# Packing the columns of two attention blocks and widening the stationary slices of the scores to 128

## The chip, the core and the metric

The kernel runs on one core of a Trainium2 chip. A core has TensorE (matrix products; a matmul keeps one operand, the stationary one, in the array and streams the other, the moving one, through it), VectorE, ScalarE, GpSimd and SyncE, an on-chip memory of 128 partitions (SBUF), accumulation banks (PSUM) and DMA queues to HBM. The profile writes them PE (TensorE's matmuls), PEld (its loads of the stationary operand), DVE (VectorE), ACT (ScalarE), POOL (GpSimd) and SP (SyncE). The metric is the device time in microseconds (us); the value before is the median of four runs. One ns is a thousandth of a us.

## The reference

Two branches read the same layer-normalised input, and their outputs are added to the input. Branch A is attention in 64 segments of 32 tokens, each with 8 memory rows that come out of the segment before. Branch B is a mixing MLP. Cut to what matters here:

```
x  = A_x                                  # [1, 2048, 1024]
xn = layernorm(x)
# branch A, for each segment s of 32 tokens, 32 heads of 128:
h = concatenate([mem, xn[segment s]])     # 8 + 32 rows
q = h @ Wq ; k = h @ Wk ; v = h @ Wv
scores = where(mask, q @ k.T * scale, -1e9)
o = softmax(scores) @ v
o = o @ Wo
mem = o[:8]                               # goes on to segment s + 1
# result
x + A(xn) + B(xn)
```

## The kernel before

The first half of the kernel (to about 755 us) computes branch B, estimates of the memory rows, and the values V of all tokens, and stores V in HBM. At lines 595 to 601 a loop over eight groups of heads does the values: matmuls on PE, and casts of the results that take turns on ACT and DVE. In the passes `hg` = 1 to 4 of that loop (lines 606 to 614) the transposed input of attention block `b = hg` is gathered into the tile `hTs`: POOL clears it (`memset`, line 612), DVE copies token columns and memory columns into it (`fill`, lines 189 and 192), and POOL's queue stores it in the HBM scratch `hT_d[b]`.

The second half is the attention proper. The 64 segments are cut into five **blocks**, 0 to 4, run one after another, each in eight passes `hg` over groups of four heads. A block is a row of **tiles** (`tiles_of`): a tile is three segments (99 columns: 96 tokens and 3 memory columns; 106 columns in the first tile of block 0) or two (66 columns). Blocks 1 and 2 have four tiles of 99, 396 columns; block 0 has 403; blocks 3 and 4 have four tiles of 99 and one of 66, 462. The number of columns of a block is `nb`, a tile's first column is `c0`, its width `T`.

Blocks 0, 3 and 4 hold their tiles side by side. Blocks 1 and 2 hold each tile of 99 in a stretch of 104 columns, 416 in all, both in the gathered input and in the tiles QT and KT of queries and keys. What of a block depends on this is `rhs` (the moving operand of the projections) and `cols` (the columns of QT and KT), lines 634 to 649.

Per pass there are three kinds of PE work in this stage:

- **Projections** (`proj`, line 667): for each of eight outputs (four heads, Q then K), eight matmuls with a 128x128 weight stationary and the block's columns moving. ACT copies the result from PSUM to QT (line 675) or KT (line 673). In blocks 1 and 2 the moving operand and the copies go through a pattern of four runs of 99.
- **Scores** (`scores`, line 682): four matmuls per tile, one for each head, with the tile's `T` query columns stationary and its `T` key columns moving. DVE adds the mask (line 684), ACT takes the exponential (686), DVE sums, inverts and normalises (688 to 694), and a transposing DMA makes PT.
- **Outputs** (`outputs`, line 706): four matmuls per tile with `T` rows of V (128 columns) stationary and `T` columns of PT moving.

A block's share of the final product with Wo (`Out.piece`, line 725: 512 moving columns) is done in pieces during the next block.

The order on PE, SP and POOL is the order in which the program issues instructions. A running clock places the small work: `tick` adds an estimate that is computed from `nb`, and issues a due scores or outputs item after a projection of eight matmuls. `step`, the distance between scores items, is computed from `nb` as well. Scores of a pass are issued after all of the projections of that pass, that is, during the projections of the next; QT and KT have two buffers each.

In all there are 2,560 projection matmuls (512 a block), 704 scores matmuls (176 tiles times four) and 704 outputs matmuls.

Of the kernel before, what the change touches and what calls it, by code (L numbers as in the profile page):

```python
# [15 lines left out]
BF16 = mybir.dt.bfloat16  # L16
# [7 lines left out]
P = 128  # L24
S = 2048
D = 1024
KT = D // P
# [50 lines left out]
def kernel(  # L78
# [16 lines left out]
    nc = tc.nc  # L95
# [14 lines left out]
    R1_v = R1_d.rearrange("(n p) d -> p n d", p=P)  # L110
    xn_d = tc.dram_tile([S, D], BF16, name="xn_scratch")
    xn_v = xn_d.rearrange("(n p) d -> p n d", p=P)
    hT_d = {b: tc.dram_tile([P, KT * c], BF16, name=f"hT{b}_scratch") for b, c in ((1, 416), (2, 416), (3, 464), (4, 464))}
    V_d = tc.dram_tile([S, H * DH], BF16, name="V_scratch")
    Vr_d = tc.dram_tile([NQ + 1, H * DH], BF16, name="Vmem_scratch")

# [77 lines left out]
    with tc.manual_schedule(engines={mybir.EngineType.PE, mybir.EngineType.SP, mybir.EngineType.Pool}), ExitStack() as actx:  # L194
# [6 lines left out]
        with ExitStack() as bctx:  # L201
# [13 lines left out]
            with ExitStack() as hctx:  # L215
# [7 lines left out]
                with ExitStack() as p0:  # L223
# [109 lines left out]
                    ps = psum.tile([P, 512], F32, tag="mm", bufs=4, name="warm")  # L333
# [52 lines left out]
                with ExitStack() as p2:  # L386
                    ring = p2.enter_context(tc.tile_pool(name="p2ring", bufs=4))
                    for n in range(NT):
                        x1 = ring.tile([P, D], F32, tag="x1")
                        st = ring.tile([P, 2, 6], F32, tag="st")  # L390
                        for ch in range(2):
                            ps = psum.tile([P, 512], F32, tag="mm", bufs=4)
                            for k in range(KT):
                                o = 2 + n * P + SH[k]
# [5 lines left out]
                        a = ring.tile([P, 1], F32, tag="a")  # L400
# [12 lines left out]
            with ExitStack() as p3:  # L413
# [118 lines left out]
                for tb in range(4):  # L532
                    depth = 1 if tb < 2 else 2
                    for f in range(FT):
                        ps = psum.tile([P, 512], F32, tag="mm", bufs=4)
# [9 lines left out]
                    if tb == 3:  # L545
                        w3ctx.close()
                        early = actx.enter_context(tc.tile_pool(name="aearly", bufs=1, side="right"))
# [3 lines left out]
                    for j in range(4):  # L551
# [8 lines left out]
                        for ch in range(2):  # L560
                            ps = psum.tile([P, 512], F32, tag="mm", bufs=4)
# [16 lines left out]
            abig = actx.enter_context(tc.tile_pool(name="abig", bufs=1))  # L578
# [4 lines left out]
            for hg in range(8):  # L583
                cs_ = slice(hg * 512, (hg + 1) * 512)
                while len(wvs) < min(8, hg + 3):
                    load_wv()
                wv = wvs[hg]
                if 1 <= hg < 5:
                    nc.gpsimd.dma_start(wo_sb[:, (hg - 1) * 8:hg * 8, :], Wo_v[:, (hg - 1) * 8:hg * 8, :])
                for m4 in range(4):  # L590
                    Vs = vsp.tile([P, 4, 512], BF16, tag="Vs")
                    for j in range(4):
                        ps = psum.tile([P, 512], F32, tag="mm", bufs=4)
                        for k in range(KT):
                            nc.tensor.matmul(ps[:], xT[:, m4 * 4 + j, k, :], wv[:, k, :], start=(k == 0), stop=(k == KT - 1))  # L595
                        if j % 2 == 0:
                            nc.scalar.copy(Vs[:, j, :], ps[:])  # L597
                            if (hg, m4, j) == (7, 3, 2):
                                nc.scalar.activation(etab[:], ps[:, 0:1], ACTF.Exp, scale=0.0)
                        else:  # L600
                            nc.vector.tensor_copy(Vs[:, j, :], ps[:])  # L601
                    nc.sync.dma_start(V_d[m4 * 512:(m4 + 1) * 512, cs_].rearrange("(j p) c -> p j c", p=P), Vs[:])
                if hg == 1:
                    for t in pns:
                        nc.gpsimd.memset(t[:], 0.0)
                if 1 <= hg < 5:
                    b, (tl, nb) = hg, tiles_of(hg)
                    if b < 3:
                        for t in tl:
                            t["c0"] = 104 * t["i"]  # L610
                    hTs = abig.tile([P, KT, 464 if b > 2 else 104 * len(tl)], BF16, tag="oX", name=f"hTs{b}")
                    nc.gpsimd.memset(hTs[:], 0.0)
                    fill(hTs, tl, lambda j, b=b: xT[:, j])
                    nc.gpsimd.dma_start(hT_d[b][:], hTs[:].rearrange("p k c -> p (k c)"))
                if hg == 6:
                    first_w = [wtile(), wtile()]
                    for w, src in zip(first_w, (Wq_v, Wk_v)):
                        nc.sync.dma_start(w[:], src[:, :, 0:512])
                if hg == 7:
                    second_w = [wtile(), abig.tile([P, KT, 512], BF16, tag="oXb", name="wk1")]  # L620
                    for w, src in zip(second_w, (Wq_v, Wk_v)):
                        nc.sync.dma_start(w[:], src[:, :, 512:1024])
                if hg == 0:
                    tl, nb = tiles_of(0)
                    hTb0 = early.tile([P, KT, 408], BF16, tag="hTb0")
                    fill(hTb0, tl, lambda j: xT[:, j])
# [6 lines left out]
        qkv = actx.enter_context(tc.tile_pool(name="aqkv", bufs=2, side="right"))  # L633
        def block_setup(b):
            tl, nb = tiles_of(b)
            ntok = sum(t["ntok"] for t in tl)
            if b == 0:
                hTb, rhs = hTb0, lambda k: hTb0[:, k, :nb]
            else:
                nt = len(tl)  # L640
                hTb = early.tile([P, KT, 464 if b > 2 else 104 * nt], BF16, tag=f"hTb{b % 2}")
                nc.gpsimd.dma_start(hTb[:].rearrange("p k c -> p (k c)"), hT_d[b][:])
                if b > 2:
                    rhs = lambda k: hTb[:, k, :nb]
                else:
                    rhs = lambda k: hTb[:, k, :].rearrange("p (t c) -> p t c", t=nt)[:, :, 0:99]
                    for t in tl:
                        t["c0"] = 104 * t["i"]
            return dict(b=b, tiles=tl, nb=nb, ntok=ntok, rhs=rhs, cols=nb if b in (0, 3, 4) else 104 * len(tl))

        def load_values(B, V, hg):
            b, cs_ = B["b"], slice(hg * 512, (hg + 1) * 512)
# [7 lines left out]
                nc.sync.dma_start(V[w:w + n, i0:i0 + k, :], Vr_d[t["r0"]:t["r0"] + n * k, cs_].rearrange("(t j) c -> j t c", j=n))  # L660

        def proj(B, w, hh, dst, scale):
            nb, nt = B["nb"], len(B["tiles"])
            flat = B["b"] in (0, 3, 4)
            ps = psum.tile([P, 512], F32, tag="mm", bufs=4)
            for k in range(KT):
                nc.tensor.matmul(ps[:, :nb] if flat else ps[:, :nb].rearrange("p (t c) -> p t c", t=nt), w[:, k, hh * P:(hh + 1) * P], B["rhs"](k), start=(k == 0), stop=(k == KT - 1))  # L667
            if flat:
                o, i = dst[:, hh, :nb], ps[:, :nb]
            else:  # L670
                o, i = dst[:, hh, :].rearrange("p (t c) -> p t c", t=nt)[:, :, 0:99], ps[:, :nb].rearrange("p (t c) -> p t c", t=nt)
            if scale is None:
                nc.scalar.copy(o, i)  # L673
            else:
                nc.scalar.mul(o, i, scale)  # L675

        def scores(t, hg, QT, KTt):
            c0, T = t["c0"], t["T"]
            psS = apsum.tile([P, 512], F32, tag="S", bufs=2)
            S3 = psS[:T, :4 * T].rearrange("p (h k) -> p h k", h=4)  # L680
            for hh in range(4):
                nc.tensor.matmul(S3[:, hh, :], QT[:, hh, c0:c0 + T], KTt[:, hh, c0:c0 + T], start=True, stop=True)  # L682
            sm = smp.tile([P, 4, 106], F32, tag="sm", bufs=3)
            nc.vector.tensor_tensor(sm[:T, :, :T], S3, t["mask"][:].unsqueeze(1).to_broadcast((T, 4, T)), op=ALU.add)  # L684
            e = sm
            nc.scalar.activation(e[:T, :, :T], sm[:T, :, :T], ACTF.Exp, scale=LN2)  # L686
            ss = sums[:T, t["gi"] * 8 + hg, :]
            nc.vector.tensor_reduce(ss, e[:T, :, :T], axis=AX.X, op=ALU.add)  # L688
            rs = smp.tile([P, 4], F32, tag="rs")
            nc.vector.reciprocal(rs[:T, :], ss)  # L690
            rows = -(-T // 16) * 16
            Pn = pns[pn_at[0] % len(pns)]
            pn_at[0] += 1
            nc.vector.tensor_tensor(Pn[:T, :, :T], e[:T, :, :T], rs[:T, :].unsqueeze(2).to_broadcast((T, 4, T)), op=ALU.mult)  # L694
            PT = smp.tile([P, 4, 112], BF16, tag="PT", bufs=5)
            PTr = PT[:].rearrange("p h q -> p (h q)")[:, :4 * rows].rearrange("p (h q) -> p h q", h=4)
            nc.sync.dma_start_transpose(PTr, Pn[:rows].rearrange("p h k -> p (h k)"))
            return PTr
# [75 lines left out]
        for gi_, group in enumerate(groups):  # L774
            Bs = [nextB[b] for b in group]
            oXs = {}
            left = [sum(len(B["tiles"]) for B in Bs) * 8]
            for hg in range(8):
# [1 line left out]
                if loads:  # L780
                    load_some(len(loads))
                wq, wk, Vs = ahead
                QTs = [qkv.tile([P, 4, B["cols"]], BF16, tag="QT", name=f"QT{B['b']}") for B in Bs]
                KTs = [qkv.tile([P, 4, B["cols"]], BF16, tag="KT", name=f"KT{B['b']}") for B in Bs]
                if hg == 2 and gi_ + 1 < len(groups):
                    nextB = {b: block_setup(b) for b in groups[gi_ + 1]}
                if hg < 7:
# [17 lines left out]
                for i, (B, t, QT, KTt, V) in enumerate(work):  # L805
# [7 lines left out]
                    oX = oXs[B["b"]][0]  # L813
                    if B["b"] == 3 and at == 384:
                        oX, at = oXs[3][1], 0
                    elif B["b"] == 4:
                        oX, at = (oXs[4][1], at) if at < P else (oX, at - P)
# [17 lines left out]
        o = outs.pop()  # L835
# [19 lines left out]
        for i in range(2):  # L855
            ps = psum.tile([P, 512], F32, tag="mm", bufs=4)
# [6 lines left out]
        flat = sums[:].rearrange("p a b -> p (a b)")  # L863
# [156 lines left out]
```

## Time and profile before

| | |
|---|---|
| median of four runs | 1515.09 us (1514.63 to 1516.51) |
| the profiled execution: its own time | 1515.09 us |
| the profiled execution: its span | 1513.0 us |
| TensorE clock granted in the span | 1.00 |
| DVE busy | 545.3 us (36%) |
| ACT busy | 504.7 us (33%) |
| POOL busy | 179.3 us (12%) |
| DMA over the span | 274.11 MB, 181 GB/s |
| attention stage | from about 755 us to the end |

The profile comes from one execution. Its span is what the profiler saw between the first and the last instruction; 2.1 us of the time lie outside of it. A matmul's duration in it goes from its start to its modelled end, and matmuls overlap: the next one starts before the end of the last. What a matmul costs a busy PE is therefore the distance from its start to the start of the next, called its **slot** below. Starts are in the trace for every matmul; slots are differences of them, and a mean of slots is over all matmuls of the kind named.

### The profile page before, as it was taken

How to read it: one execution, taken by the hardware profiler on the slowest of the kernel's cores; microseconds unless marked ns; L12 is line 12 of the kernel's file. 1: busy time of each engine (PE TensorE's matmuls, PEld its weight loads, DVE VectorE, ACT ScalarE, POOL GpSimd, SP SyncE). 2: the span in 40 equal slices, each digit the busy share in tenths (PEclk: the TensorE clock that was granted, in tenths of full speed). 3: DMA queues.
4: the chain of work that ended last, by engine and by line, in shares of the span. 5: the costliest groups of instructions: out<-in, count | busy, mean ns of one | idle time of the engine just before them, and what ended most of it. 6: DMA issues, size and time to landing. Idle time of an engine off the chain costs nothing.

```text
span 1513.0 us, 24367 instructions
## 1 busy us (share of the span) xinstructions
PE 1506.7 (100%) x9850; PEld 807.7 (53%) x9850; DVE 545.3 (36%) x1138; ACT 504.7 (33%) x1142; POOL 179.3 (12%) x248
## 2 busy tenths in 40 slices
PE   9999999999999999999999999999999999999998
PEld 7844444445444444444466645664665455545555
DVE  8382230100020122222246624651564166516642
ACT  6533203013012011111256614650663266406630
POOL 5241020211111231100000010001000100010001
PEclk9999999999999999999999999999999999999999
DMA  8699752453345887532399946992998298918811
GB/s 295 147 253 336 220 177 89 136 202 112 125 163 146 196 277 253 205 120 84 126 244 242 247 124 182 247 239 70 243 245 203 72 228 224 216 60 212 190 46 53
DMA packets 303539, 274.11 MB, mean 181 GB/s; under 512 B 153926, under 2 KB 270184, under 8 KB 303424
## 3 DMA queue, kind: packets, MB, share of 16 engines
q1 hardware_dynamic: 281248, 189.92, 50.1%
q0 software_dynamic: 22032, 82.54, 15.7%
q8 instruction: 79, 1.29, 0.4%
q14 instruction: 36, 0.29, 0.1%
q10 hardware_dynamic: 144, 0.07, 0.0%
HBM read 190.93 MB, written 46.14 MB: 157 GB/s over the span
## 4 chain that ended last, share of the span: by engine, by line
PE 99%; DMA 1%; ACT 0%; DVE 0%; SPq 0%; issue 0%
PE ps L667 30%; PE pso L725 15%; PE ps L595 15%; PE ps L537 13%; PE ps L563 13%; PE ps L395 4%; PE ps L318 3%; PE psS L682 2%; PE psO L706 2%; PE ps L860 1%; PE ps L487 1%; PE gps L466 0%; PE ps L452 0%; DMA PT<-Pn 0%; DMA xt<-in_A_x_dram 0%; PE ps L308 0%
## 5 line engine op out<-in xcount | busy, mean ns | idle before, releaser
L667 PE MATMUL ps<-hTb,wt 128*128 128x396 bf16 (+2 forms) x2528 | 497.6, 343 | 0.0
L667 PEld LDWEIGHTS <-wt 128*128 128x128 bf16 x2528 | 232.7, 98 | 166.6 <-DMA wt<-in_A_Wq_dram 0.3
L595 PE MATMUL ps<-wt,xT 128*128 128x512 bf16 x1024 | 221.2, 379 | 0.0
L725 PE MATMUL pso<-wo_sb,oX 128*128 128x512 bf16 (+1 forms) x992 | 210.9, 372 | 0.0
L537 PE MATMUL ps<-xn3T,w_sb 128*128 128x512 bf16 x896 | 196.2, 379 | 0.0
L563 PE MATMUL ps<-w_sb,h3T 128*128 128x512 bf16 x896 | 195.5, 379 | 0.0
L595 PEld LDWEIGHTS <-xT 128*128 128x128 bf16 x1024 | 100.2, 98 | 120.8
L538 ACT ACTIVATE h3T<-ps 128x512 bf16<-128x512 f32 x112 | 66.9, 597 | 290.3 <-PE ps L537 289.4
L725 PEld LDWEIGHTS <-oX 128*128 128x128 bf16 x992 | 96.1, 98 | 106.5
L673 ACT CAST KT<-ps 128x462 bf16<-128x462 f32 (+2 forms) x160 | 82.1, 513 | 190.8 <-PE ps L667 187.8
L563 PEld LDWEIGHTS <-h3T 128*128 128x128 bf16 x896 | 87.0, 98 | 103.3
L537 PEld LDWEIGHTS <-w_sb 128*128 128x128 bf16 x896 | 86.5, 98 | 102.1
L688 DVE TENSOR_REDUCE sums<-sm 99x4 f32<-99x396 f32 (+2 forms) x176 | 97.6, 555 | 113.4 <-ACT sm L686 113.4
L675 ACT ACTIVATE QT<-ps 128x462 bf16<-128x462 f32 (+2 forms) x160 | 84.1, 526 | 113.1 <-PE ps L667 100.3
L597 ACT CAST Vs<-ps 128x512 bf16<-128x512 f32 x64 | 37.5, 586 | 233.2 <-PE ps L595 233.2
L684 DVE TENSOR_TENSOR sm<-psS,c_mask_reg_sb 99x396 f32<-99x396 f32 x152 | 86.7, 570 | 76.8 <-PE psS L682 76.8
L686 ACT ACTIVATE sm<-sm 99x396 f32<-99x396 f32 (+2 forms) x176 | 92.9, 528 | 58.9 <-DVE sm L684 54.0
L601 DVE CAST Vs<-ps 128x512 bf16<-128x512 f32 x64 | 44.3, 692 | 170.0 <-PE ps L595 168.7
L694 DVE TENSOR_TENSOR Pn<-sm,rs 99x396 bf16<-99x396 f32 (+2 forms) x176 | 98.9, 562 | 7.6 <-DMA PT<-Pn 1.5
L564 DVE TENSOR_TENSOR R<-ps,R 128x512 f32<-128x512 f32 x32 | 21.9, 689 | 181.6 <-PE ps L563 167.8
L732 POOL DMA_DIRECT2D out_dram<-ot x30 | 16.4, 546 | 587.6 <-DVE ot L731 581.7
L731 DVE TENSOR_TENSOR ot<-pso,Rt 128x512 bf16<-128x512 f32 (+1 forms) x33 | 22.3, 675 | 171.6 <-PE pso L725 166.3
(124 smaller groups left out, 1072.1 us busy)
## 6 DMA issues: line engine op xcount, KB each, us to landing
wt<-in_A_Wq_dram SPq DMA_DIRECT2D x76, 512.0 KB
wt<-in_A_Wk_dram SPq DMA_DIRECT2D x76, 512.0 KB
wt<-in_A_Wv_dram POOLq DMA_DIRECT2D x24, 1024.0 KB, 6.5
V_scratch<-Vs SPq DMA_DIRECT2D x32, 512.0 KB
V<-V_scratch SPq DMA_DIRECT2D x40, 384.0 KB
R_scratch<-x POOLq DMA_DIRECT2D x16, 512.0 KB, 4.4
R<-R_scratch SPq DMA_DIRECT2D x16, 512.0 KB
R_scratch<-R POOLq DMA_DIRECT2D x16, 512.0 KB, 3.2
```

Source lines behind the costliest of these rows:

```text
L537: nc.tensor.matmul(ps[:].rearrange("p (n t) -> p n t", t=P), w3_sb[:, k, f * P:(f + 1) * P], xn3T[tb][:, :, k, :], start=(k == 0), stop=(k ...
L538: nc.scalar.activation(h3T[:, f, :], ps[:], ACTF.Gelu_apprx_tanh)
L563: nc.tensor.matmul(ps[:], h3T[:, f, j * P:(j + 1) * P], w4_sb[:, f, ch * 512:(ch + 1) * 512], start=(f == 0), stop=(f == FT - 1))
L595: nc.tensor.matmul(ps[:], xT[:, m4 * 4 + j, k, :], wv[:, k, :], start=(k == 0), stop=(k == KT - 1))
L667: nc.tensor.matmul(ps[:, :nb] if flat else ps[:, :nb].rearrange("p (t c) -> p t c", t=nt), w[:, k, hh * P:(hh + 1) * P], B["rhs"](k), star ...
L673: nc.scalar.copy(o, i)
L675: nc.scalar.mul(o, i, scale)
L684: nc.vector.tensor_tensor(sm[:T, :, :T], S3, t["mask"][:].unsqueeze(1).to_broadcast((T, 4, T)), op=ALU.add)
L686: nc.scalar.activation(e[:T, :, :T], sm[:T, :, :T], ACTF.Exp, scale=LN2)
L688: nc.vector.tensor_reduce(ss, e[:T, :, :T], axis=AX.X, op=ALU.add)
L694: nc.vector.tensor_tensor(Pn[:T, :, :T], e[:T, :, :T], rs[:T, :].unsqueeze(2).to_broadcast((T, 4, T)), op=ALU.mult)
L725: nc.tensor.matmul(self.ps[:, :self.w], self.oX[0][:, h, self.oX[1] + self.gl * P:self.oX[1] + (self.gl + 1) * P], wo_sb[:, h, self.cc], s ...
```

## The change

First, blocks 1 and 2 lose their padding. Their scratch in HBM has 396 columns in place of 416, `hTs` and `hTb` have `nb` columns, tiles start at multiples of 99 instead of 104, QT and KT have `nb` columns, and the projection's matmul and the two ACT copies use one flat run of columns in every block. `rhs`, `cols` and the two cases in `proj` go.

Second, in every block the stationary operand of a scores matmul is 128 query columns wide instead of `T`. The heads of QT are read as one flat row of `4 * nb` columns, and the slice begins at the tile's first column of the head, so it goes on into the columns of the next tile or the next head. The result has 128 rows in PSUM; only the first `T` are read afterwards. Where fewer than 128 columns are left in the flat row, the slice keeps the width `T`: the last head of a block's last tile.

```diff
-    hT_d = {... for b, c in ((1, 416), (2, 416), (3, 464), (4, 464))}
+    hT_d = {... for b, c in ((1, 396), (2, 396), (3, 464), (4, 464))}
...
-                    if b < 3:
-                        for t in tl:
-                            t["c0"] = 104 * t["i"]
-                    hTs = abig.tile([P, KT, 464 if b > 2 else 104 * len(tl)], BF16, tag="oX", name=f"hTs{b}")
+                    hTs = abig.tile([P, KT, 464 if b > 2 else nb], BF16, tag="oX", name=f"hTs{b}")
...
-                hTb = early.tile([P, KT, 464 if b > 2 else 104 * nt], BF16, tag=f"hTb{b % 2}")
+                hTb = early.tile([P, KT, 464 if b > 2 else nb], BF16, tag=f"hTb{b % 2}")
                 nc.gpsimd.dma_start(hTb[:].rearrange("p k c -> p (k c)"), hT_d[b][:])
-                if b > 2:
-                    rhs = lambda k: hTb[:, k, :nb]
-                else:
-                    rhs = lambda k: hTb[:, k, :].rearrange("p (t c) -> p t c", t=nt)[:, :, 0:99]
-                    for t in tl:
-                        t["c0"] = 104 * t["i"]
-            return dict(b=b, tiles=tl, nb=nb, ntok=ntok, rhs=rhs, cols=nb if b in (0, 3, 4) else 104 * len(tl))
+            return dict(b=b, tiles=tl, nb=nb, ntok=ntok, hT=hTb)
...
-                nc.tensor.matmul(ps[:, :nb] if flat else ps[:, :nb].rearrange("p (t c) -> p t c", t=nt), w[:, k, hh * P:(hh + 1) * P], B["rhs"](k), start=(k == 0), stop=(k == KT - 1))
+                nc.tensor.matmul(ps[:, :nb], w[:, k, hh * P:(hh + 1) * P], B["hT"][:, k, :nb], start=(k == 0), stop=(k == KT - 1))
...
+            qf = QT[:].rearrange("p h c -> p (h c)")
+            nb = QT.shape[2]
             for hh in range(4):
-                nc.tensor.matmul(S3[:, hh, :], QT[:, hh, c0:c0 + T], KTt[:, hh, c0:c0 + T], start=True, stop=True)
+                a = hh * nb + c0
+                w = P if a + P <= 4 * nb else T
+                nc.tensor.matmul(psS[:w, hh * T:(hh + 1) * T], qf[:, a:a + w], KTt[:, hh, c0:c0 + T], start=True, stop=True)
...
-                QTs = [qkv.tile([P, 4, B["cols"]], BF16, tag="QT", name=f"QT{B['b']}") for B in Bs]
-                KTs = [qkv.tile([P, 4, B["cols"]], BF16, tag="KT", name=f"KT{B['b']}") for B in Bs]
+                QTs = [qkv.tile([P, 4, B["nb"]], BF16, tag="QT", name=f"QT{B['b']}") for B in Bs]
+                KTs = [qkv.tile([P, 4, B["nb"]], BF16, tag="KT", name=f"KT{B['b']}") for B in Bs]
```

More of the change, by code (lines that the diff above doesn't have):

```diff
@@ L112 @@
     xn_v = xn_d.rearrange("(n p) d -> p n d", p=P)
-    hT_d = {b: tc.dram_tile([P, KT * c], BF16, name=f"hT{b}_scratch") for b, c in ((1, 416), (2, 416), (3, 464), (4, 464))}
+    hT_d = {b: tc.dram_tile([P, KT * c], BF16, name=f"hT{b}_scratch") for b, c in ((1, 396), (2, 396), (3, 464), (4, 464))}
     V_d = tc.dram_tile([S, H * DH], BF16, name="V_scratch")
@@ L637, in block_setup @@
             if b == 0:
-                hTb, rhs = hTb0, lambda k: hTb0[:, k, :nb]
+                hTb = hTb0
             else:
-                nt = len(tl)
-                hTb = early.tile([P, KT, 464 if b > 2 else 104 * nt], BF16, tag=f"hTb{b % 2}")
+                hTb = early.tile([P, KT, 464 if b > 2 else nb], BF16, tag=f"hTb{b % 2}")
                 nc.gpsimd.dma_start(hTb[:].rearrange("p k c -> p (k c)"), hT_d[b][:])
-                if b > 2:
-                    rhs = lambda k: hTb[:, k, :nb]
-                else:
-                    rhs = lambda k: hTb[:, k, :].rearrange("p (t c) -> p t c", t=nt)[:, :, 0:99]
-                    for t in tl:
-                        t["c0"] = 104 * t["i"]
-            return dict(b=b, tiles=tl, nb=nb, ntok=ntok, rhs=rhs, cols=nb if b in (0, 3, 4) else 104 * len(tl))
+            return dict(b=b, tiles=tl, nb=nb, ntok=ntok, hT=hTb)
         def load_values(B, V, hg):
@@ L662, in proj @@
         def proj(B, w, hh, dst, scale):
-            nb, nt = B["nb"], len(B["tiles"])
-            flat = B["b"] in (0, 3, 4)
+            nb = B["nb"]
             ps = psum.tile([P, 512], F32, tag="mm", bufs=4)
             for k in range(KT):
-                nc.tensor.matmul(ps[:, :nb] if flat else ps[:, :nb].rearrange("p (t c) -> p t c", t=nt), w[:, k, hh * P:(hh + 1) * P], B["rhs"](k), start=(k == 0), stop=(k == KT - 1))
-            if flat:
-                o, i = dst[:, hh, :nb], ps[:, :nb]
-            else:
[L671 to L675, printed above, removed]
+                nc.tensor.matmul(ps[:, :nb], w[:, k, hh * P:(hh + 1) * P], B["hT"][:, k, :nb], start=(k == 0), stop=(k == KT - 1))
+            if scale is None:
+                nc.scalar.copy(dst[:, hh, :], ps[:, :nb])
+            else:
+                nc.scalar.mul(dst[:, hh, :], ps[:, :nb], scale)
         def scores(t, hg, QT, KTt):
```

## The prediction

> **What bounds the kernel now.** I read the page's busy rows first, then the chain that ended last, then the groups kept apart by shape, then PE in order of time.
>
> ```profile
> PE 1506.7 (100%) x9850; PEld 807.7 (53%) x9850; DVE 545.3 (36%) x1138; ACT 504.7 (33%) x1142; POOL 179.3 (12%) x248
> PE 99%; DMA 1%; ACT 0%; DVE 0%; SPq 0%; issue 0%
> PE ps L667 30%; PE pso L725 15%; PE ps L595 15%; PE ps L537 13%; PE ps L563 13%; PE ps L395 4%; PE ps L318 3%; PE psS L682 2%; PE psO L706 2%; PE ps L860 1%; PE ps L487 1%; PE gps L466 0%; PE ps L452 0%; DMA PT<-Pn 0%; DMA xt<-in_A_x_dram 0%; PE ps L308 0%
> ```
>
> PE has work for the whole span, and the chain is PE's own queue. Nobody else sets the end, so a change is worth what it takes from PE's slots. The lines that it touches are L667 (30%) and L682 (2%).
>
> Groups by shape: instructions, then busy us and mean ns of one, then idle us before them.
>
> ```profile
> L667 PE MATMUL ps<-hTb,wt 128*128 128x462 bf16 x1024 | 217.3, 358 | 0.0
> L667 PE MATMUL ps<-hTb,wt 128*128 128x396 bf16 x1024 | 193.1, 332 | 0.0
> L682 PE MATMUL psS<-KT,QT 128*99 128x99 bf16 x608 | 53.4, 210 | 0.0
> L706 PE MATMUL psO<-PT,V 99*128 99x99 bf16 x608 | 51.9, 207 | 0.5 <-DMA PT<-Pn 0.5
> L682 PEld LDWEIGHTS <-QT 128*99 128x99 bf16 x608 | 47.9, 127 | 12.8
> L706 PEld LDWEIGHTS <-V 99*128 99x128 bf16 x608 | 43.2, 97 | 26.6 <-PE ps L667 0.8 <-issue 0.3
> L395 PEld LDWEIGHTS <-hTB 128*128 128x128 bf16 x256 | 25.1, 98 | 30.0
> L682 PEld LDWEIGHTS <-QT 128*66 128x66 bf16 x64 | 4.1, 112 | 1.5
> ```
>
> The reader is to see three things. No touched PE group waits for anything worth counting. A load of 99 columns takes longer (127 ns) than one of 128 (97 or 98). And L682 and L706 are near twins: both stream 99 columns, and differ in the width of the load.
>
> These durations overlap, so the cost is read from PE's order of time in block 1 (start, length, work):
>
> ```profile
> 942.14 0.35 PE L682 MATMUL psS<-KT,QT 128*99 128x99 bf16 x4
> 942.33 1.52 PE L667 MATMUL ps<-hTb,wt 128*128 128x396 bf16 x8
> 943.68 0.34 PE L706 MATMUL psO<-PT,V 99*128 99x99 bf16 x4
> 943.86 1.52 PE L667 MATMUL ps<-hTb,wt 128*128 128x396 bf16 x8
> 945.22 0.35 PE L682 MATMUL psS<-KT,QT 128*99 128x99 bf16 x4
> ```
>
> From start to start, four scores cost 0.19 us, eight projections 1.35, four outputs 0.18. Finer means come from the start times of the single matmuls:
>
> | matmul | slot, ns |
> |---|---|
> | projection, four runs of 99 (after another projection) | 169.1 |
> | projection, 403 and 462 in one run (medians) | 171 and 195 |
> | 512 in one run (L563) and as four runs of 128 (L537) | 215.9 and 215.9 |
> | scores, tiles of three segments: head 0 after a projection | 43.9 |
> | the same, heads 1, 2, 3 | 47.0, 47.5, 47.3 |
> | outputs, the same tiles, heads 1, 2, 3 | 43.4, 43.5, 43.5 |
> | scores of 66, heads 1, 2, 3 | 31.6, 32.7, 32.4 |
> | outputs of 66, heads 1, 2, 3 | 29.4, 29.2, 29.1 |
>
> Head 0's load lies behind a projection of 169 ns; heads 1 to 3 have theirs behind a matmul of 43. So the narrow load shows exactly where it has no long matmul to lie behind.
>
> **Part 1, one flat run in blocks 1 and 2.** 2 x 512 = 1,024 projections go from four runs to one. PE streams 2.4 columns a ns: (215.9 - 195) / (512 - 462) is 0.418 ns a column. From the flat 462, 396 columns cost 195 - 66 x 0.417 = 167.5; from 403, 171 - 7 x 0.417 = 168.1. Runs of 128 cost no more than one run of 512, so it is not the pattern that costs: 169.1 is what 400 columns would, each odd run of 99 being paid as 100. The 403 run is odd too, so I take 167.5. Gain: 1,024 x (169.1 - 167.5) = **1.6 us**; ends 1,024 x 1.0 = 1.0 and 1.75. The lower end is for rows that start at multiples of 792 bytes, where flat ones started at multiples of 816 or 928 so far.
>
> A first projection after narrow scores takes 170.0 ns in these blocks, 0.9 more than after a projection; there are 63 of them: 0.06 us more.
>
> **Part 2, 128 columns.** The wide load should behave like that of V. 136 to 176 of each of heads 1 to 3 change: 176 tiles, less 40 last heads of last tiles (five blocks by eight passes) that stay narrow. By the outputs' slots the three-segment tiles give 160 x (3.6 + 4.0) + 128 x 3.8 ns = 1.70 us and the two-segment ones 16 x (2.2 + 3.5) + 8 x 3.3 = 0.12: 1.8 us. Head 0 gains nothing.
>
> But the outputs stream from aligned starts, and scores' keys will mostly not. Head 0 after a projection shows what that costs once the load is hidden: 43.45 ns where the keys start at a multiple of four columns (62 cases), 44.6 elsewhere (26 cases), so 1.2 more. With tiles at multiples of 99, three in four starts are of the second kind: 0.75 x 1.2 = 0.9 ns on each of some 490 widened matmuls, 0.4 us, which the narrow load has hidden; and in blocks 1 and 2, whose keys all start at multiples of 104 now, also on 48 heads 0: 0.06 us. I take this, since it is the same instruction: **1.4 us**; ends 0.9 (the 1.2 at its largest group, 2.0) and 1.9.
>
> **A rule against the change.** The Trainium skill, "TensorE: Matmul & The Clock Gate", section LDWEIGHTS, has a load's time grow with its columns, P / 1.2 ns: 82 for 99, 107 for 128, so 24 ns more; laid open on 664 widened loads, 16 us slower. The trace has it the other way round (127 against 98). The same page, section on weight-path modes, states a fast load that is on when the stationary operand is exactly 128 wide and not FP32; that agrees with the rows of 66, 99, 106 and 128 columns: 112, 127, 129, 98. I take the rows. Do odd starts lose it? Half of L395's loads start one column off an even one: 98 ns, like the rest. That row lies behind 512-column matmuls, so it shows no slot.
>
> **What costs nothing, and what hides it.** The copies to QT and KT: 503 and 492 ns for four runs of 99, 509 and 498 for 403 flat, the same by the column; ACT is at 33%. The gather of blocks 1 and 2 goes to odd columns, as that of 3 and 4 does: 350 ns for 96 tokens in both, and PE's 512-column slots beside it stay at 215.8. POOL's clear gets 5% shorter (2,895 ns for 3,328 columns), and the DMA to and from the scratch as well; the scratch is read at pass 2 of the block before, tens of us ahead. The wide slice reads columns of other heads, but Q is done before K, and the scores wait for K's last copy anyway: no new wait. Without that cover a pass would wait for an ACT copy, about 0.5 us by 40 passes. No instruction moves: the clock uses `nb`, which stays 396. POOL and SP keep their order.
>
> **Sum.** 1.6 + 0.06 + 1.4 = 3.05 us off a span of 1513.0, so 1510.0, and with 2.1 outside 1512.0; the profiled execution is the median one. That is 0.20%, and about 0.2% is what a measurement of this kernel can tell from no change.
>
> **Rivals.**
>
> - *Both parts in full*: no price for odd key starts, and 1.75 for the flat run: 1.9 + 0.06 + 1.75 = 3.7, 1511.4. For: the outputs' 43.4, the even width of 396. Against: 44.6 in 26 heads 0.
> - *Only the flat run pays*: the extra 4 ns of heads 1 to 3 are then a price of loads behind short matmuls whatever their width, and wide ones pay it too: 1.6, so 1513.5. Against: the outputs, loaded at 128, pay no such thing.
> - *Nothing*: flat odd rows at 792 bytes are paid like the padded runs: 1515. Against: 403 and 462.
> - *Slower*: the wide slice from the middle of QT gets no fast load, and a slow one grows with its width: 32.2 ns for 66 and 47.3 for 99 make 0.46 a column, 60.5 at 128. Then 448 slots lose 13.2 and 40 lose 28.3: 7.0 us, less 1.6: 5.4 slower, 1520.5. For: V and the weights start at aligned columns, and L395's slots can't show it. Against: L395's duration. It decides from (3.0 + 1.6) / 488 = 9.5 ns a slot on.
>
> **Chances.** Forecast, 2.5 to 3.5 us off, 0.56, in halves on each side of 0.2%; both in full 0.20; only the flat run 0.12; nothing 0.04; slower 0.08. Faster by over 0.2%: 0.28 + 0.20, and 0.02 for more than any case; same: 0.28 - 0.02 + 0.12 + 0.04; slower 0.08. The range leaves out slower and half of nothing: from 1510.5 (in full, and 0.9 for the scatter of the runs) to 1514.3.
>
> **What would show it.** Loads of L682 at 97 or 98 ns but for 40; slots of heads 1 to 3 near 44; projections of blocks 1 and 2 at 167.5; the cycle of 16 projections, four scores and four outputs in block 1, 3.07 us from 942.14 to the next like it, at 3.04; L667 still without idle time. Wrong if the loads stay over 120 ns, if the flat slot stays at 169, or if PE waits for a copy.

## The result, and the profile after

| | before | changed |
|---|---|---|
| median, us | 1515.36 (60 runs) | 1513.22 (40 runs) |
| ratio, 95% interval | | 0.9986 [0.9982, 0.9991] |
| span of the profiled execution, us | 1513.0 | 1510.7 |

The changed kernel is 2.1 us, or 0.14%, faster. That is less than the 3.05 us that were forecast, and less than the 0.2% named there as what a measurement tells from no change; with this many runs the interval still lies clear of 1. Line numbers move: the projections are at 656, the scores at 671, the outputs at 695, the product with Wo at 714.

The page of the changed kernel: PE's busy row and the chain that ended last.

```profile
PE 1503.6 (100%) x9850; PEld 803.4 (53%) x9850; DVE 545.4 (36%) x1138; ACT 503.8 (33%) x1142; POOL 178.7 (12%) x248
PE 99%; DMA 1%; ACT 0%; DVE 0%; SPq 0%; issue 0%
PE ps L656 30%; PE pso L714 15%; PE ps L595 15%; PE ps L537 13%; PE ps L563 13%; PE ps L395 4%; PE ps L318 3%; PE psO L695 2%; PE psS L671 2%; PE ps L849 1%; PE ps L487 1%; PE gps L466 0%; PE ps L452 0%; DMA PT<-Pn 0%; DMA xt<-in_A_x_dram 0%; PE ps L308 0%
```

PE still bounds the kernel, and no other engine has come into the chain. The groups of the changed kernel by shape (instructions, busy us and mean ns of one, idle us before them):

```profile
L656 PE MATMUL ps<-hTb,wt 128*128 128x462 bf16 x1024 | 217.2, 358 | 0.0
L656 PE MATMUL ps<-hTb,wt 128*128 128x396 bf16 x1024 | 192.3, 330 | 0.0
L695 PE MATMUL psO<-PT,V 99*128 99x99 bf16 x608 | 51.9, 207 | 0.3 <-DMA PT<-Pn 0.3
L671 PE MATMUL psS<-KT,QT 128*128 128x99 bf16 x576 | 50.5, 207 | 0.0
L671 PEld LDWEIGHTS <-QT 128*128 128x128 bf16 x664 | 44.1, 98 | 17.2
L671 PEld LDWEIGHTS <-QT 128*99 128x99 bf16 x32 | 4.0, 125 | 0.0
L671 PEld LDWEIGHTS <-QT 128*66 128x66 bf16 x8 | 0.9, 114 | 0.0
```

The 664 wide loads take 98 ns, and exactly the 40 expected ones stayed narrow at 125 and 114. A scores matmul now lasts what an outputs matmul does, 207 ns. PE in order of time in block 1 (start, length, work):

```profile
941.44 0.34 PE L671 MATMUL psS<-KT,QT 128*128 128x99 bf16 x4
941.61 1.51 PE L656 MATMUL ps<-hTb,wt 128*128 128x396 bf16 x8
942.96 0.34 PE L695 MATMUL psO<-PT,V 99*128 99x99 bf16 x4
943.14 1.51 PE L656 MATMUL ps<-hTb,wt 128*128 128x396 bf16 x8
944.49 0.34 PE L671 MATMUL psS<-KT,QT 128*128 128x99 bf16 x4
```

Four scores went from 0.19 to 0.17 us. The cycle went from 3.07 to 3.05, where 3.04 was expected. The slots (differences of start times, as before) say which part is short. The sums are over all matmuls of a kind:

| | before | changed | forecast |
|---|---|---|---|
| projections, block 1, us | 86.70 | 86.41 | 85.9 |
| projections, block 2, us | 86.72 | 86.42 | 85.9 |
| all scores, us | 32.17 | 30.75 | 30.8 |
| projection, even k / odd k (k from 2 on), ns | 169 / 169 | 167 / 170 | 167.5 |
| scores of three-segment tiles, heads 1, 2, 3, ns | 47.0, 47.5, 47.3 | 44.2, 44.8, 45.0 | near 44 |

Scores gave 1.42 us, as forecast. The flat run gave 0.6 us, where the forecast had 1.6. The two make 2.0, and the medians differ by 2.1. (The two profiled spans differ by 2.3; another 0.3 of that is shorter waits in block 0.) In the changed kernel the eight `k` of a projection alternate: even `k` take 167 ns, odd ones 170. A row of 396 columns is 792 bytes, so in the gathered input, counted from the start of the tile, row `k` starts at a multiple of 16 bytes for even `k`, and 8 bytes past one for odd `k`.

### The profile page after: what moved, and what is told of

It reads as the page before. It is cut to its first block, busy times and chain, and to the rows that moved or that the text cites. A ratio compares the mean times of both kernels' runs of the same rounds, so it can differ in the third digit from the quotient of the medians.

```text
span 1510.7 us, 24367 instructions
## 1 busy us (share of the span) xinstructions
PE 1503.6 (100%) x9850; PEld 803.4 (53%) x9850; DVE 545.4 (36%) x1138; ACT 503.8 (33%) x1142; POOL 178.7 (12%) x248
## 4 chain that ended last, share of the span: by engine, by line
PE 99%; DMA 1%; ACT 0%; DVE 0%; SPq 0%; issue 0%
PE ps L656 30%; PE pso L714 15%; PE ps L595 15%; PE ps L537 13%; PE ps L563 13%; PE ps L395 4%; PE ps L318 3%; PE psO L695 2%; PE psS L671 2%; PE ps L849 1%; PE ps L487 1%; PE gps L466 0%; PE ps L452 0%; DMA PT<-Pn 0%; DMA xt<-in_A_x_dram 0%; PE ps L308 0%
## 5 line engine op out<-in xcount | busy, mean ns | idle before, releaser
L720 DVE TENSOR_TENSOR ot<-pso,Rt 128x512 bf16<-128x512 f32 (+1 forms) x33 | 22.3, 675 | 171.6 <-PE pso L714 166.2
```

## The experiments

**Each part alone.** The first kernel takes the wide slices back and keeps the packing:

```diff
-                w = P if a + P <= 4 * nb else T
+                w = T
```

> The packed columns of blocks 1 and 2 alone: the scores keep stationary slices of T columns. If the parts are separate, as read from the slots: loads of the scores back at 125 to 128 ns, scores slots in sum back from 30.7 to about 32.2 us, projections of blocks 1 and 2 as in the changed kernel (86.4 us a block, odd k at 170, even k at 167 ns), and a span 0.6 to 0.9 us below that of the kernel before. Rival, that the wide loads bring the slots of the projections down or up as well: the projections of blocks 1 and 2 change by over 0.2 us a block against the changed kernel.

The second keeps the wide slices and packed QT and KT, and goes back to four runs of 99 out of 104 for the projections of blocks 1 and 2:

```diff
-                nc.tensor.matmul(ps[:, :nb], ..., B["hT"][:, k, :nb], ...)
+                rhs = B["hT"][:, k, :].rearrange("p (t c) -> p t c", t=4)[:, :, 0:99] if four else B["hT"][:, k, :nb]
+                o = ps[:, :nb].rearrange("p (t c) -> p t c", t=4) if four else ps[:, :nb]
+                nc.tensor.matmul(o, ..., rhs, ...)
```

> The wide slices alone: the projections of blocks 1 and 2 again stream four runs of 99 out of stretches of 104, QT and KT stay packed, so that the keys start where they do in the changed kernel. If the scores' gain is the wide load's: loads at 98 ns, scores in sum 30.7 us, projections of blocks 1 and 2 back at 86.7 us a block with all k at 169, and a span 1.4 to 1.7 us below that of the kernel before. Rival, that a part of the scores' gain comes from the packed projections beside them: scores in sum over 31.2 us.

Loads of the scores by shape, in the packing-only kernel and in the wide-only kernel (where they are at line 677):

```profile
L671 PEld LDWEIGHTS <-QT 128*99 128x99 bf16 x608 | 47.9, 127 | 12.7
```

```profile
L677 PEld LDWEIGHTS <-QT 128*128 128x128 bf16 x664 | 44.2, 98 | 17.3
```

| | packing only | wide only | changed |
|---|---|---|---|
| median, us (before, run beside them: 1515.22) | 1514.33 | 1513.99 | |
| ratio to before | 0.9994 [0.9985, 1.0002] | 0.9993 [0.9984, 1.0001] | 0.9986 [0.9982, 0.9991] |
| projections, blocks 1 and 2, us | 86.43, 86.46 | 86.71, 86.72 | 86.41, 86.42 |
| all scores, us | 32.09 | 30.79 | 30.75 |

Each part leaves the other's slots alone: the packing is worth 0.6 us with or without wide slices, the wide slices 1.4 with or without packed projections. The medians stand 0.9 and 1.2 us below the kernel before, together 2.1, the size of the whole change; each interval alone still holds 1, so it is the slots that separate the parts. So in the slots both expectations held, and both rivals fell. In time the packing met its 0.6 to 0.9 by the medians, and the wide slices' 1.2 is a little short of their 1.4 to 1.7.

**Where a row starts.** The next kernel gives a row of the gathered input 400 columns, 800 bytes, of which 396 are streamed. Nothing else changes:

```diff
-    ... ((1, 396), (2, 396), (3, 464), (4, 464))
+    ... ((1, 400), (2, 400), (3, 464), (4, 464))
...
-                hTb = early.tile([P, KT, 464 if b > 2 else nb], ...)
+                hTb = early.tile([P, KT, 464 if b > 2 else 400], ...)
```

(`hTs` likewise.)

> As the changed kernel, but the rows of the gathered input of blocks 1 and 2 have 400 columns (800 bytes, a multiple of 16) with 396 used. Theory, the start of an odd row at 8 bytes past a multiple of 16 costs what was missing from the forecast: odd and even k at 167 to 167.6 ns, 85.4 to 85.8 us a block in place of 86.4, and a span 1.2 to 2.0 us below the changed kernel's, 3.4 to 4.2 below that of the kernel before. Rival, that the alternation belongs to odd k or to a run of 396 columns and not to where the row starts: odd k stay at 170 ns, 86.4 us a block, and the span is that of the changed kernel.

The same stretch of block 1 with rows of 400 columns, in order of time, and below it the group:

```profile
941.49 0.34 PE L671 MATMUL psS<-KT,QT 128*128 128x99 bf16 x4
941.66 1.50 PE L656 MATMUL ps<-hTb,wt 128*128 128x396 bf16 x8
943.00 0.34 PE L695 MATMUL psO<-PT,V 99*128 99x99 bf16 x4
943.18 1.50 PE L656 MATMUL ps<-hTb,wt 128*128 128x396 bf16 x8
944.52 0.34 PE L671 MATMUL psS<-KT,QT 128*128 128x99 bf16 x4
```

```profile
L656 PE MATMUL ps<-hTb,wt 128*128 128x396 bf16 x1024 | 191.4, 331 | 0.0
```

The cycle is 3.03 us now. All `k` but the first of a group stand between 167.0 and 167.5 ns, and a block's projections at 85.81 and 85.82 us: 0.9 us a block below the kernel before. Over both blocks that is 1.8 us, the forecast's 1.6 and a little more: the slots behind another projection went from 169.1 to 167.4, and the first of a group gained some 2 ns. The alternation went with the starts, not with odd `k` and not with the run of 396. The median was 1512.39 us, the ratio 0.9982 [0.9973, 0.9990]. The slots came out as expected and the time did not: the median is 2.8 us below the kernel before, where 3.4 to 4.2 were expected of the span.

**Other starts.** With rows of 397 columns (794 bytes), every `k` starts at another place:

```diff
-    ... ((1, 396), (2, 396), (3, 464), (4, 464))
+    ... ((1, 397), (2, 397), (3, 464), (4, 464))
```

> As the changed kernel with rows of 397 columns (794 bytes) for blocks 1 and 2, so that the eight k start at 0, 10, 4, 14, 8, 2, 12 and 6 bytes past a multiple of 16. If the start alone decides: the slots of the eight k differ, k 0 cheapest, and the dear ones show the grain: with 16 bytes, most of the seven others at about 170; with 8 bytes and odd rows paid as one more grain, k 0 and 4 alike and below the others. Rival, that odd k is what costs: 170 for k 1, 3, 5, 7 and 167 for the others whatever the start.

| k | 0 | 1 | 2 | 3 | 4 | 5 | 6 | 7 |
|---|---|---|---|---|---|---|---|---|
| start, bytes past a multiple of 16 | 0 | 10 | 4 | 14 | 8 | 2 | 12 | 6 |
| slot in block 1, ns | 168.9 | 171.6 | 170.2 | 171.0 | 170.2 | 167.5 | 170.5 | 170.9 |

(`k` 0 holds the first projections after outputs, which cost 4 ns more.) Six of the seven others are dear. Odd `k` is not what costs, since `k` 2, 4 and 6 are dear here. Nor is it a grain of 8 bytes: `k` 4, at 8, is as dear as the others. Whether a start 2 bytes past is cheap in itself stays open, since a slot can also take time from its neighbours: the even `k` of the changed kernel stand at 166.7, below the 167.4 of rows that are all aligned. The sums are surer. Against rows of 400, a group of eight costs 9 ns more with rows of 396 and 20 ns more with rows of 397. A block's projections took 87.10 and 87.13 us, more than with the padded runs of the kernel before (a single run of each kernel: 1516.17 beside 1515.02). Packing one column worse would have made the first part a loss.

**Width 120.** The wide slices of the tiles of 99 are cut to 120 columns:

```diff
-                w = P if a + P <= 4 * nb else T
+                w = (120 if T == 99 else T) if a + P <= 4 * nb else T
```

> As the changed kernel, but the stationary slices of the scores of the tiles of 99 are 120 columns wide in place of 128. If the fast load needs exactly 128 columns: loads of 120 take over 127 ns, and heads 1 to 3 of these tiles take more than the 47.3 ns of the kernel before, 53 to 57, some 3 us in all above the kernel before's scores. Rival, that a wide slice is cheap [...]: loads and slots as with 128, 98 ns and 44 to 45 ns.

The loads by shape, and PE in order of time in block 1, in the kernel with slices of 120:

```profile
L671 PEld LDWEIGHTS <-QT 128*120 128x120 bf16 x576 | 51.1, 134 | 12.0
L671 PEld LDWEIGHTS <-QT 128*106 128x106 bf16 x32 | 2.4, 129 | 0.2
L671 PEld LDWEIGHTS <-QT 128*99 128x99 bf16 x32 | 4.1, 127 | 0.0
L671 PEld LDWEIGHTS <-QT 128*66 128x66 bf16 x64 | 4.1, 112 | 1.5
```

```profile
938.93 1.52 PE L656 MATMUL ps<-hTb,wt 128*128 128x396 bf16 x8
940.28 0.37 PE L671 MATMUL psS<-KT,QT 128*120 128x99 bf16 x4
940.49 1.51 PE L656 MATMUL ps<-hTb,wt 128*128 128x396 bf16 x8
```

Loads grow with their width up to 120 columns (112, 127, 129, 134 ns) and drop to 98 at 128. The trace records them in two forms as well: every load of 128 reads its columns as four runs of 32, every narrower one (66, 99, 106, 120) as one run. Four scores take 0.21 us from start to start. Slots of heads 1 to 3 behind loads of 120 are about 55 ns, and all scores took 36.02 us, 3.9 more than before the change. The time of its single run was 4.7 us above that of the kernel before beside it; the scores' 3.9 less the packing's 0.6 explain 3.3 of it, and 0.9 more lies in three long slots of projections in block 4 (0.32, 0.32 and 0.83 us in place of 0.20 each). So it is the full 128 that pays, and the rule of the Trainium skill ("TensorE: Matmul & The Clock Gate", section on weight-path modes: fast when exactly 128 wide) holds here, while its P / 1.2 (section LDWEIGHTS) has only the direction of the narrow loads' growth, at twice the 0.4 ns a column that 112 to 134 ns for 66 to 120 columns make.

**Starts of keys and queries.** To the kernel with rows of 400, one adds keys in stretches of 104 in blocks 1 and 2, the other does the same to the queries as well, and POOL clears their unused columns:

```diff
-                nc.scalar.copy(dst[:, hh, :], ps[:, :nb])
+                nc.scalar.copy(dst[:, hh, :].rearrange("p (t c) -> p t c", t=4)[:, :, 0:99], ps[:, :nb].rearrange("p (t c) -> p t c", t=4))
...
-                nc.tensor.matmul(..., KTt[:, hh, c0:c0 + T], ...)
+                nc.tensor.matmul(..., KTt[:, hh, ck:ck + T], ...)
```

```diff
-                QTs = [qkv.tile([P, 4, B["nb"]], ...)]
+                QTs = [qkv.tile([P, 4, 416 if B["b"] in (1, 2) else B["nb"]], ...)]
...
+                        nc.gpsimd.memset(q[:].rearrange("p h (t c) -> p (h t) c", c=104)[:, :, 99:104], 0.0)
...
-                a = hh * nb + c0
+                a = hh * nb + ck
```

> As the kernel with rows of 400 columns, and the keys of blocks 1 and 2 lie in stretches of 104 columns, so that every moving slice of the scores there starts at a multiple of 16 bytes; the queries stay packed. Theory, the odd start of the keys costs about 1 ns on each of three in four scores: scores of blocks 1 and 2 at 5.57 us a block in place of 5.68 (heads 1 to 3 at 43.5 ns but for the last, narrow one), 0.2 us in all, and K's copies on ACT are as long as before. Rival, that what is left above 43.5 ns in heads 1 to 3 comes from the stationary slice's start and not from the keys': 5.66 to 5.70 us a block.

> As the kernel with rows of 400 columns and keys in stretches of 104, and the queries of blocks 1 and 2 lie in stretches of 104 too, so that their stationary slices of 128 also start at a multiple of 16 bytes; POOL clears the five unused columns of each stretch (one small memset a pass), since the slices run over them. If the half ns that heads 1 to 3 still stand above the outputs' 43.5 is the stationary slice's start: heads 1 to 3 at 43.5 ns, scores of blocks 1 and 2 at 5.60 us a block in place of 5.68. Rival, that starts have no part in it and it is what scores cost with their waits: 5.66 to 5.70 us a block. In both cases the projections stay at 85.8 us a block, and the time stays within 0.3 us of the kernel with aligned keys; if ACT's copies come to wait for the memset and PE for them, PE shows idle time before the scores and the time goes up.

Scores of blocks 1 and 2 took 5.68 us a block with aligned keys, and 5.68 with aligned queries as well; 5.68 in the changed kernel, and 5.72 with rows of 400 alone. With all starts aligned, heads 1 to 3 stand evenly at 43.9 to 44.4 ns (but for the narrow last one); without, single slots go from 43 to 47.6, and the sum is the same to 0.04 us a block. The figures of both rivals held, though the first rival's reason, the start of the queries, fell with the second kernel: starts move time between neighbouring slots and cost nothing that the sum shows. What the half ns and more above the outputs' 43.5 is stays open. Waits are not it: in the kernel with all starts aligned, heads 1 and 2 of blocks 1 and 2 stand at 44.1 ns whether their matmul waits for or sends a signal (29 cases) or neither (99). The ratios to before were 0.9975 [0.9966, 0.9985] and 0.9978 [0.9968, 0.9987].

**The three side by side.** The changed kernel and the two best were run once more on one chip:

> The changed kernel once more, beside the two with rows of 400 columns on one chip. It should stand 2.0 to 2.4 us below the kernel before, as its slots do (0.6 us from the projections of blocks 1 and 2, 1.4 us from the scores).

> Rows of 400 columns once more, beside the changed kernel on one chip. If the projections' 1.2 us (86.4 to 85.8 us in each of two blocks) are on the path, it is 1.0 to 1.5 us below the changed kernel. Rival, that they are given back elsewhere: within 0.4 us of it.

> Rows of 400 columns and keys in stretches of 104 once more. By the slots of the first run (scores of blocks 1 and 2 at 5.68 against 5.72 us a block) it is 0.1 us below the kernel with rows of 400 alone, which the times can't tell from none; if the 0.6 us between the two medians of the first run were real, it is that much below again.

| | median, us | ratio to before (1515.06) |
|---|---|---|
| changed | 1513.16 | 0.9989 [0.9980, 0.9997] |
| rows of 400 | 1512.37 | 0.9977 [0.9970, 0.9985] |
| rows of 400, keys in 104 | 1512.09 | 0.9980 [0.9972, 0.9987] |

(The ratios are not quotients of the medians.) The changed kernel lies 1.9 us below the kernel before, just short of the 2.0 to 2.4 expected. Rows of 400 lie 0.8 us below it, between the 1.0 to 1.5 of the theory and the 0.4 of its rival; the slots of these executions again show the full 1.2 (86.41 and 86.43 to 85.81 and 85.82). PE's waits in the attention stage show where some of it may go: the changed kernel of this series first, then the rows of 400 (waits in us, times, longest).

```profile
PE psO L695 <- DMA PT<-Pn: 0.2, 1, 0.2
```

```profile
PE psO L695 <- DMA PT<-Pn: 1.0, 2, 0.5
```

Outputs waited twice for the transposing DMA of PT in the second of these executions, 0.8 us longer in all. It is one execution of each; other executions of these three kernels show 0.2 to 0.9 us of waits before outputs. So a part given back in this wait is seen, but its usual size isn't settled. The two kernels with rows of 400 can't be told apart. Both are below the changed kernel in median and in fastest run (1511.58 and 1511.34 against 1512.50), while their intervals against the kernel before overlap its interval.

## Why the prediction was right and where it was off

- **What bounds the kernel.** Right. The slots' sums give the change in time to a few tenths of a us.
- **Part 2, 128 columns.** Right in size, 1.42 us against 1.4, and right that the width is the cause. The loads, the 40 narrow ones and the slots near 44 came as forecast; the kernel with the wide slices alone shows that they are enough, and the one with 120 columns that the width is the cause. That 1.4 was met and not the twin's 1.8 is in part luck. The forecast charged odd starts of the keys with 1.2 ns, from 26 heads 0 (and 1.8 less 0.4 and 0.06 is nearer to 1.3); with all keys aligned the scores still took 5.68 us a block. Single slots do move with the start, and I took a mean of them for a cost. What kept heads 1 to 3 above the twin's slots is something else, and is open. A further 0.1 us came where the forecast had "Head 0 gains nothing": the eight heads 0 that follow outputs of 66 columns went from 61.1 to 48.5 ns. By the forecast's own reason they could have been counted, since their load lies behind a matmul of 29 ns. The 50 that follow outputs of 99 gained nothing (48.4 and 48.3).
- **Part 1, one flat run.** This is the term that was mis-sized: "From the flat 462, 396 columns cost 195 - 66 x 0.417 = 167.5" gave 1.6 us, and 0.6 was measured, below the lower end of 1.0 that was put on "rows that start at multiples of 792 bytes". By the forecast's own measure, a projection after another projection, the slot went from 169.1 to 168.7 and not to 167.5, which comes near to its sign of being wrong, that "the flat slot stays at 169". The rows that the 167.5 came from start at multiples of 816 and 928 bytes, all multiples of 16; 792 is not one. With 800 bytes the 167.5 is met. So the arithmetic on columns was right for aligned rows, and the place of the risk was named, but the risk was sized at 0.6 ns a matmul (1.0 in place of 1.6 us over 1,024) and is 1.2 ns in the mean (0.6 us over the 512 of a block).
- **The rule against the change**, with its estimate of 16 us slower, fell as forecast: no widened load grew (98 ns), and the scores' slots got shorter.
- **Covers.** Held: ACT's copies to QT and KT in blocks 1 and 2 took 500 and 488 ns (503 and 492 before), the gather 358 ns at most (355), POOL's clear 2,760 ns for 3,168 columns; the projections and scores of PE show no wait.
- **Rivals.** "Only the flat run pays" and "slower" fell with the loads at 98 ns. "Both in full" would have needed the aligned rows for its flat run; its 1.9 for the scores came in no kernel, 1.4 with aligned keys (30.77 us in all). "Nothing" was closest to what happened to Part 1: two thirds of its gain were indeed eaten by the rows at 792 bytes.
- **The number.** 3.05 less the 1.0 that Part 1 lacked is 2.05 us; measured 2.1. The time of 1513.22 us lies inside the stated range, 1510.5 to 1514.3, which reached so far up for the cases with a smaller gain.

## What to carry to other kernels

When padding is removed, look at where each row of the result starts, not only at how many columns are streamed: 1.2 of the 1.8 us were lost to rows of 792 bytes and came back with four unused columns a row. A stationary operand a little narrower than 128 is worth widening to exactly 128 if neighbouring data can be read harmlessly and its loads lie behind matmuls too short to hide them (43 ns here); 120 is worse than 99 here. A mean of slots over a few cases, picked by what stands ahead of them, is no price: compare sums over whole groups, since neighbouring slots lend each other time.

## What the runs showed of the hardware

- Moving rows of 396 columns: 167.0 to 167.5 ns when all start at multiples of 16 bytes; with every second row 8 bytes past one, slots alternate between 170 and 167, 9 ns more on a group of eight; with seven of eight rows off such a start, six slots stand at 170 to 172, 20 ns more on a group. Finer prices of single starts aren't known.
- Four runs of 99 columns, each from an aligned start, take 169.1 ns, some 1.6 more than 396 columns in one aligned run. Why is not shown: the forecast's reading, an odd run paid as one column more, fits (403 columns in one run take 170.8 ns, as 404 would), but no run varied it.
- A stationary operand of 128 columns loads in 98 ns, and narrower ones of 66, 99, 106 and 120 columns in 112, 127, 129 and 134. Behind a matmul of 99 columns, a matmul of 99 with a load of 99, 120 or 128 columns takes about 47, 55 or 44 ns.
- The first matmul after a switch between 128 and 99 active rows takes about 4 ns more: the first output after a projection 48 ns where the next three take 43.5, the first projection after outputs 173 where others take 169, and in blocks 3 and 4 199 where others take 195 (all in the kernel before). Between scores and projections, both of 128 rows, there is no such step. Every switch here goes to or from outputs, so that it is the rows and nothing else of the outputs is not shown.
